# Re-ordering the queues of a fused convolution and two-layer product: multiplications of the taps, the order of the adds, the seeds of the next step, and the list of the first product

## The chip, the cores and the metric

The kernel runs on one core of a Trainium2 chip. Five engines matter. PE multiplies matrices and writes to PSUM; VectorE (DVE) adds, subtracts and transposes; ScalarE (ACT) copies, scales and applies the activation; GpSimd (POOL) adds and issues DMAs that accumulate; SyncE (SP) issues the other DMAs. Each engine works through its own queue in the order in which the program emitted the instructions, and waits on semaphores for the others. The metric is the device time of one execution in microseconds (us), lower is better; the time shown for a kernel is the median of its runs.

## The reference

```python
# x: (8, 4096, 192), weight: (8, 7), w_in: (192, 2048), w_out: (2048, 192), all float32
w = softmax(weight, axis=-1)                      # 7 taps for each of 8 heads
out = sum over k of w[h, k] * x_pad[b, s + k, h, :]  # causal: 6 zeros ahead of x
x = out.reshape(32768, 192)
h = x @ w_in
g = h * (1 / (1 + exp(-1.702 * h)))
return g @ w_out                                  # (32768, 192)
```

A causal convolution with seven taps is followed by two matrix products with a sigmoid-gated activation between them.

## The kernel before, in words

**Steps.** The 32768 rows are worked off in 32 steps (`big`), each of two times 512 rows from two halves of the batch. In step `big` the kernel does the first product and the second product of that step, and beside them it prepares the convolution of step `big + 2`. Steps 2 to 29 have all of this; step 0 is written out apart (`first_step`), step 1 has lists of its own (`FILL_1`), and the last two steps have no convolution left to prepare.

**First product** (`hidden`, L763, called with `v` = 0 and `v` = 1). It does not multiply block by block: 20 products (`TERMS`) replace 24, at the price of sums and copies. `FIRST` (L643) is the list of this work, written out by hand: a `prod` is four matrix instructions (L595, two halves of 64 rows in two passes each), a `copy` is two ACT copies of 128x512 (L630), a `sum` is two DVE additions or subtractions (L636), a `gelu` is two ACT activations from PSUM (L612) or one from SBUF (L617). Names a0 to a9 stand for pairs of PSUM banks, of which there are four; a pair is taken from a list of free ones when its name first occurs and put back at its last use. Names k0 to k6 stand for the five buffers `room`, by the table `ROOM_OF` (L658, one row for each `v`). An item marked 1 or 2 in front belongs to the next half: with `v` = 0 it is work for `v` = 1, with `v` = 1 it is work for the next step. For those of mark 1 that means: they are kept in `later` and emitted when the next step begins (`rest_ahead`, L733), so the order of products on PE in a step is 0, 4, 10, 6, 2, 13, 18, then the list for `v` = 0 with 14, 17, 3, 16, 1 and so on, then the list for `v` = 1. The first of them, the copy of a0 to a2, is the seed of the next step: product 0 adds to that copy. It is emitted still within the second product, where `PLAN` has `final` (`final`, L1315, through `seeds_ahead`, L725).

**Fillers.** `FILL` (L660) says between which items of `FIRST` other work is emitted: `add` (POOL additions of 128x512 of a multiplied tap to the convolution, `next_add` L501), `turn` (DVE transposes of x), `vsum` (POOL sums of blocks of the convolution, L363 and L361), `g` (DVE sums of blocks of g), `cross` (SP DMAs that copy blocks of the convolution to the other 64 rows, L523). At the first `turn` all adds that are left are emitted, and the DMA `cross` of one block.

**Second product** (`second`, L1002). 20 main products with four steps each (two for one of them) are worked through in 78 rounds (`go`, L1036); a round is three matrix instructions of the main product and one of a side product, in two passes, so eight instructions of L1020. `PLAN` (L954) is the list, in which the rounds stand between everything else: `sum` (DVE, 128x1024, L361 and L363), `acc` (POOL DMAs that accumulate, L996), `seed` (ACT copy 96x256, L1049), `join` (DVE 96x256), `turn` (DVE transpose, L935), `store` (SP, L946), `tap` (one ACT multiplication of x by a tap, 128x512, L487), `tree` (POOL DMAs that add up the taps of one third of the columns, L509). When a side product is complete, ACT copies it out of PSUM at once (32x256, L1045). 21 taps are multiplied in a step; those of two thirds of the columns are added by the 12 POOL additions of the next step, in the order in which they were multiplied (first in, first out).

**What sets the order.** Nothing is planned at run time. Emission order is queue order on each engine, and an instruction waits for the last writers and readers of what it touches. At the boundary of two steps the program emits, in this order: side copy after round 74, two more rounds, the seed (`final`), two rounds, the last side copy, then `rest_ahead` with product 0, product 4, the copy of a2 to k2, product 10, the copy of a0 to k6, the sum that makes a4, and so on.

Of the kernel before, what the change touches and what calls it, by code (L numbers as in the profile page):

```python
# [15 lines left out]
def kernel(  # L16
# [80 lines left out]
    g = consts.tile([P, NG, 2, 2, NG, T], F32)  # L97
# [401 lines left out]
    tree, adds = [], []  # L499

    def next_add():  # L501
        if adds:
            dst, home = adds.pop(0)
            nc.gpsimd.tensor_add(dst, dst, home)  # L504

    def add_taps():
# [57 lines left out]
    def prepare(big):  # L564

        for k in range(K if big < 3 else 0):
            yield "", 0.76 if k else 0.48, lambda k=k: conv(big, 1, k)
        yield f"conv {big}", 0.0, lambda: None
        def done():
            need(f"taps {big}")  # L570
            while adds:
                next_add()
            if OPEN_SUM:
                sums_c(big, *OPEN_SUM)
            cross(big, OPEN, OPEN + 1)

        yield f"done {big}", 0.0, done
# [60 lines left out]
    def plain(u, m, n, v, slot, ks=range(NC), first=0):  # L638

        for k in ks:  # L640
            product1(slot, NC * (2 * u + m) + k, 2 * k + n, 0, v, k == first)

    FIRST = [  # L643
# [13 lines left out]
    ]  # L657
    ROOM_OF = ((0, 4, 1, 1, 4, 4, 4), (3, 0, 2, 2, 0, 2, 1))  # L658

    FILL = [  # L660
        {
            1: (("add", 4), ("add", 4), ("add", 4)), 9: (("turn", 0),), 15: (("turn", 1),), 21: (("turn", 2),),
        },
        {
            0: (("vsum",), ("vsum",), ("vsum",), ("vsum",)), 1: (("vsum",),), 2: (("vsum",),), 3: (("g", 0),),
            12: (("g", 1),), 13: (("g", 2), ("vsum",)), 17: (("g", 3), ("vsum",), ("vsum",)), 18: (("g", 4),),
            20: (("vsum",),), 26: (("vsum",),),
        },
    ]
    FILL_1 = [  # L670
        {
            0: (("add", 12),), 7: (("work", 0.8),), 10: (("tap",), ("work", 0.8)), 13: (("tap",),),
            15: (("work", 0.8),), 19: (("tap",),), 25: (("work", 0.8),), 29: (("work", 0.8), ("tap",)),
            32: (("work", 0.8),), 35: (("tap",),), 36: (("tap",),), 40: (("tap",),), 42: (("work", 0.8),),
        },
        {
            3: (("g", 0),), 13: (("g", 1),), 16: (("g", 2),), 17: (("g", 3),), 22: (("g", 4),), 29: (("turn", 0),),
            31: (("turn", 1),), 35: (("turn", 2),),
        },
    ]  # L680

# [9 lines left out]
    def do(big, v, half, kind, *args):  # L691
# [7 lines left out]
        def at(name):  # L699
            return where[name] if name[0] == "a" else rooms[ROOM_OF[v][int(name[1:])]]  # L700

# [236 lines left out]
    def store(big, n, o=None, queues=(nc.sync,) * 3):  # L938
# [13 lines left out]
        (6, 6, "-", 10), (0, 5, "+", 6), (8, 8, "+", 0), (1, 7, "-", 6), (1, 1, "-", 11),  # L952
    ]
    PLAN = [  # L954
        ("sum", 14, 14, "-", 18), ("side", 13, 16, "k0"), ("main", 1, 5, "p2", 1), ("vsum",), ("cross",), ("go", 3),
# [16 lines left out]
        ("main", 9, 6, "p4", 0), ("vsum",), ("go", 1), ("tap",), ("tap",), ("tap",), ("go", 2),  # L972
        ("join", "k9", "p1", "+", "k5"), ("go", 1), ("join", "k10", "p0", "-", "k9"), ("main", 3, 15, "p2", 0),
        ("go", 1), ("acc", 18, 14), ("tree",), ("go", 1), ("seed", "p1", "k1", 1), ("sum", 5, 7, "+", 15), ("go", 2),
        ("main", 21, 7, "p2", 0), ("tap",), ("tap",), ("tap",), ("go", 1), ("sum", 6, 14, "+", 6), ("go", 1),
        ("side", 7, 20, "k1"), ("vsum",), ("vsum",), ("tree",), ("go", 1), ("tap",), ("go", 1), ("sum", 6, 6, "-", 17),
# [13 lines left out]
        ("turn", 1, 1, 0, "k8"), ("store", 1, 0),  # L990
    ]

    def sum_g(dst, a, op, b=None):
# [358 lines left out]
```

## Time and profile before

| what | value |
| --- | --- |
| median of three runs | 2308.58 us (2307.7 to 2309.06) |
| the profiled execution | 2306.48 us |
| its span, first to last instruction | 2304.7 us |
| PE busy | 2267.7 us, 98% |
| DVE busy | 1935.8 us, 84% |
| ACT busy | 1779.9 us, 77% |
| POOL busy | 1069.3 us, 46% |
| granted TensorE clock | 0.998 |
| copies of side products, ACT L1045 | 364 ns each, 651 of them |
| taps, ACT L487 | 714 ns each, 534 in the largest group |
| adds of taps, POOL L504 | 1312 ns each, 354 of them |

The span is what the engines need from the first to the last instruction; 1.78 us of the profiled execution's time lie around it. Busy time is a share over the whole execution, and PE is busy nearly always. In such a kernel the shares say little. What counts is where PE is late, by how much in one step, and who let it go, since the same pattern is repeated in 28 steps. In a line of the timeline stand the start, the busy time, the engine, the line of the code, the operation, what it writes and reads, the shapes, the count, and in brackets how long the engine idled before it and who released it. In the chain of waits stand the pieces of work that set the end, with start and length.

### The profile page before, as it was taken

The page shows a single profiled execution, that of the slowest core. Times are in us where ns is not written, and L with a number is a line of the kernel's source. Part 1 is how long each engine was busy: PE and PEld are TensorE (multiplying, and loading weights), DVE is VectorE, ACT ScalarE, POOL GpSimd, SP SyncE. Part 2 cuts the span into 40 slices and gives each one's busy share as a digit, 9 for nine tenths or more (in the row PEclk, how much of TensorE's full clock was granted, in tenths as well). Part 3 has the DMA queues.
Part 4 walks back from the last instruction along what each step waited for, and adds up shares of the span by engine and source line. Part 5 has one row for each costly group of instructions (what it writes and reads, how often), then busy time and mean ns, then how long its engine had stood idle before and what let it go on. Part 6 is the DMA issues. An engine that isn't in the chain of part 4 may idle for free.

```text
span 2304.7 us, 62266 instructions
## 1 busy us (share of the span) xinstructions
PE 2267.7 (98%) x24966; PEld 1343.7 (58%) x24966; DVE 1935.8 (84%) x2842; ACT 1779.9 (77%) x3481; POOL 1069.3 (46%) x1101
## 2 busy tenths in 40 slices
PE   9899999999999999999999999999999999999999
PEld 4356556665556556566565566565556555655655
DVE  8798888888888888888888888788888788888788
ACT  8578877778777788777788777887777877778755
POOL 1446544555444554535554445555355544455510
PEclk9999999999999999999999999999999999999999
DMA  8876667666676666676666766666766667664543
GB/s 199 156 150 134 130 118 154 128 127 124 126 139 135 132 123 131 119 150 130 126 130 122 140 138 128 123 129 119 152 127 126 128 119 147 135 131 97 101 96 70
DMA packets 281073, 298.85 MB, mean 130 GB/s; under 512 B 120144, under 2 KB 212304, under 8 KB 280784
## 3 DMA queue, kind: packets, MB, share of 16 engines
q0 software_dynamic: 58080, 151.48, 36.5%
q1 hardware_dynamic: 221056, 143.00, 27.6%
q8 instruction: 197, 3.23, 0.6%
q14 instruction: 92, 0.75, 0.1%
q10 hardware_dynamic: 1648, 0.39, 0.1%
HBM read 53.15 MB, written 25.17 MB: 34 GB/s over the span
## 4 chain that ended last, share of the span: by engine, by line
PE 82%; ACT 11%; DVE 5%; issue 2%; DMA 1%; SPq 0%; POOL 0%; DVEq 0%; ACTq 0%; POOLq 0%
PE slot L595 47%; PE slot L1020 34%; ACT g L487 6%; ACT room L1045 2%; PE slot L837 1%; DVE g L363 1%; DVE slot L361 1%; ACT room L1049 0%; DMA conv_t<-conv_t 0%; DVE g L361 0%; DVE room L361 0%; ACT slot L1049 0%; ACT g L612 0%; DVE room L363 0%; DMA osbs<-in_moe_w_out_dram 0%
## 5 line engine op out<-in xcount | busy, mean ns | idle before, releaser
L595 PE MATMUL slot<-conv_t,w_in_s 64*128 64x512 f32 x5152 | 1159.6, 598 | 12.6 <-issue 8.1
L595 PEld LDWEIGHTS slot<-conv_t,w_in_s 64*128 64x128 f32 x5152 | 700.8, 186 | 460.5 <-issue 209.7
L1020 PE MATMUL slot<-g,w_form 128*32 128x256 f32 x9672 | 900.1, 379 | 0.3 <-DVE room L363 0.3
L1020 PEld LDWEIGHTS slot<-g,w_form 128*32 128x32 f32 x9672 | 482.1, 110 | 160.2 <-DVE room L363 0.8
L636 DVE TENSOR_TENSOR slot<-slot,room 128x512 f32<-128x512 f32 x496 | 321.7, 694 | 205.6 <-ACT g L612 132.1
L612 ACT ACTIVATE g<-slot 128x512 f32<-128x512 f32 x776 | 429.2, 610 | 78.9 <-PE slot L595 78.6
L1020 PE MATMUL slot<-g,w_out_s 128*32 128x256 f32 x5952 | 468.1, 380 | 9.5 <-DVE slot L361 5.6
L504 POOL TENSOR_TENSOR conv_t<-conv_t,g 128x512 f32<-128x512 f32 x354 | 463.1, 1312 | 23.1
L363 DVE TENSOR_TENSOR g<-g 128x1024 f32<-128x1024 f32 x372 | 449.6, 1229 | 5.3
L1045 ACT COPY room<-slot 32x256 f32<-32x256 f32 x651 | 236.8, 364 | 252.2 <-PE slot L1020 242.4
L630 ACT COPY room<-slot 128x512 f32<-128x512 f32 x620 | 340.2, 597 | 65.1 <-PE slot L595 34.1
L1020 PEld LDWEIGHTS slot<-g,w_out_s 128*32 128x32 f32 x5952 | 237.1, 110 | 210.2 <-ACT g L617 23.5
L487 ACT ACTIVATE g<-xt,cw 128x512 f32<-128x512 f32 x534 | 347.7, 714 | 3.7
L509 POOL DMA_DIRECT2D g<-g x120 | 120.8, 1025 | 322.4 <-DVE room L361 140.9
L996 POOL DMA_DIRECT2D g<-g x124 | 116.2, 937 | 295.2 <-DVE g L363 209.7
L363 POOL TENSOR_TENSOR conv_t<-conv_t 128x256 f32<-128x256 f32 x210 | 163.2, 787 | 185.6 <-PE slot L595 185.3
L1020 PE MATMUL slot<-osbs,w_form 128*32 128x256 f32 x2232 | 227.3, 379 | 0.2 <-ACT room L1049 0.2
L636 DVE TENSOR_TENSOR slot<-room,slot 128x512 f32<-128x512 f32 x248 | 159.7, 690 | 26.6 <-PE slot L595 24.3
L630 ACT COPY slot<-slot 128x512 f32<-128x512 f32 x248 | 135.7, 576 | 41.2 <-PE slot L595 40.2
L636 DVE TENSOR_TENSOR room<-slot,room 128x512 f32<-128x512 f32 x248 | 159.1, 682 | 5.3 <-ACT room L630 2.1
L617 ACT ACTIVATE g<-room 128x1024 f32<-128x1024 f32 x124 | 132.7, 1070 | 38.2 <-DVE room L636 38.2
L1020 PEld LDWEIGHTS slot<-osbs,w_form 128*32 128x32 f32 x2232 | 113.9, 110 | 42.7 <-ACT room L1049 0.6
(171 smaller groups left out, 1744.2 us busy)
## 6 DMA issues: line engine op xcount, KB each, us to landing
g<-g POOLq DMA_DIRECT2D x124, 512.0 KB, 5.8
xin<-in_x_dram SPq DMA_DIRECT2D x240, 180.0 KB, 4.1
conv_t<-conv_t SPq DMA_DIRECT2D x186, 192.0 KB, 2.9
g<-g POOLq DMA_DIRECT2D x120, 256.0 KB, 5.5
out_dram<-osbs SPq DMA_DIRECT2D x186, 128.0 KB, 2.5
conv_t<-conv_t SPq DMA_DIRECT2D x124, 128.0 KB, 2.3
g<-room POOLq DMA_DIRECT2D x31, 512.0 KB, 5.1
conv_t<-g POOLq DMA_DIRECT2D x60, 256.0 KB, 6.0
```

The lines of the kernel that those rows point to most:

```text
L363: eng.tensor_sub(v(dst), v(a), v(b))
L487: act.mul(home, conv_src(big, c, k), cw[:, c, k : k + 1])
L504: nc.gpsimd.tensor_add(dst, dst, home)
L509: nc.gpsimd.dma_start(out=out, in_=src, accum_op=ALU.add)
L595: nc.tensor.matmul(slot[h], w_in_s[halves[h], a, v * P : (v + 1) * P], src, start=first, stop=True, skip_group_check=True,)
L612: act.activation(dst[:, :, h, :], src[h].rearrange("p (o t) -> p o t", o=2), AF.Gelu_apprx_sigmoid, scale=float(sign),)
L617: act.activation(dst.rearrange("p o h t -> p h o t"), src.rearrange("p h (o t) -> p h o t", o=2), AF.Gelu_apprx_sigmoid, scale=float(sign),)
L630: act.copy(bank(dst, h), bank(src, h))
L636: op(*(bank(t, h) for t in (dst, a, b)))
L996: nc.gpsimd.dma_start(out=spot(dst), in_=spot(a), accum_op=ALU.add)
L1020: nc.tensor.matmul(dst, w, t, start=first, stop=last, skip_group_check=True)
L1045: act.copy(to, d)
```

## The change

Five things change, all of them positions in lists. The instructions are the same in number, shape and kind.

1. `next_add` takes the last entry of the list of adds and not the first. The POOL additions of a step come in the opposite order: the tap that was multiplied last is added first.
2. In `FIRST` products 5 and 19 change places, the copy to k3 and the activation of a7 change places, and the sum that makes a3 stands at the head of the list. By the order in which names take free bank pairs, a3 then takes the pair that a9 left and a1 the one that a0 left, where it was the other way round.
3. `ROOM_OF` puts k5 of `v` = 0 into buffer 1 (it was 4) and k6 of `v` = 1 into buffer 4 (it was 1).
4. `FILL` and `FILL_1` place adds, transposes of x, sums of blocks, and sums of g elsewhere. The first sum of g for `v` = 1 comes behind the sum that makes a3. One `cross` moves from `PLAN` to `FILL`.
5. In `PLAN` the taps are placed anew, DVE sums and POOL accumulations move by some rounds, and `final` stands two rounds earlier, behind round 74, with the last tap behind it.

```diff
-            dst, home = adds.pop(0)
+            dst, home = adds.pop()
...
-        (0, "prod", 1, "a1"), (0, "gelu", 1, 0, "a5", 1), (0, "prod", 15, "a6"), (0, "prod", 7, "a4"),
-        (0, "copy", "a7", "a6", 1), (0, "gelu", 1, 1, "a4", 1), (0, "prod", 19, "a6"),
-        (0, "sum", "a8", "a1", "-", "k2"), (0, "prod", 5, "a7"), (0, "prod", 12, "a8"), (0, "copy", "k3", "a6", 1),
-        (0, "sum", "k4", "a8", "+", "k3"), (0, "gelu", 0, 1, "a7", 1), (2, "prod", 11, "a0"),
...
+        (0, "sum", "a3", "a4", "-", "k1"), (0, "gelu", 2, 1, "a0", 1), (0, "copy", "k0", "a2", 1),
+        (0, "prod", 14, "a1"), (0, "prod", 17, "a3"), (0, "sum", "a5", "k1", "-", "a1"), (0, "gelu", 3, 1, "a3", 1),
...
+        (0, "prod", 15, "a6"), (0, "prod", 7, "a4"), (0, "gelu", 1, 0, "a5", 1), (0, "copy", "a7", "a6", 1),
+        (0, "prod", 5, "a7"), (0, "prod", 19, "a6"), (0, "gelu", 1, 1, "a4", 1), (0, "gelu", 0, 1, "a7", 1),
+        (0, "sum", "a8", "a1", "-", "k2"), (0, "prod", 12, "a8"), (2, "prod", 11, "a0"), (0, "copy", "k3", "a6", 1),
...
-    ROOM_OF = ((0, 4, 1, 1, 4, 4, 4), (3, 0, 2, 2, 0, 2, 1))
+    ROOM_OF = ((0, 4, 1, 1, 4, 1, 4), (3, 0, 2, 2, 0, 2, 4))
...
-            1: (("add", 4), ("add", 4), ("add", 4)), 9: (("turn", 0),), 15: (("turn", 1),), 21: (("turn", 2),),
+            0: (("add", 4),), 6: (("add", 4),), 7: (("turn", 0),), 9: (("add", 4),), 21: (("turn", 1),),
+            26: (("turn", 2),),
...
-            0: (("vsum",), ("vsum",), ("vsum",), ("vsum",)), 1: (("vsum",),), 2: (("vsum",),), 3: (("g", 0),),
+            0: (("vsum",),), 1: (("vsum",), ("vsum",)), 2: (("g", 0),), 6: (("vsum",), ("vsum",)), 8: (("vsum",),),
...
-        ("main", 9, 6, "p4", 0), ("vsum",), ("go", 1), ("tap",), ("tap",), ("tap",), ("go", 2),
+        ("main", 9, 6, "p4", 0), ("vsum",),
+        ("tap",), ("go", 2), ("tap",), ("go", 1), ("join", "k9", "p1", "+", "k5"), ("tree",), ("go", 1),
...
-        ("main", 21, 7, "p2", 0), ("tap",), ("tap",), ("tap",), ("go", 1), ("sum", 6, 14, "+", 6), ("go", 1),
+        ("sum", 5, 7, "+", 15), ("go", 1), ("main", 21, 7, "p2", 0), ("tap",), ("tap",), ("tap",), ("tap",), ("go", 1),
...
-        ("store", 0, 0), ("main", 24, 19, "p5", 0), ("go", 2), ("final",), ("join", "k1", "p3", "-", "k3"), ("go", 1),
+        ("turn", 1, 0, 0, "k6"), ("store", 0, 0), ("main", 24, 19, "p5", 0), ("final",), ("tap",), ("go", 2),
+        ("join", "k1", "p3", "-", "k3"), ("go", 1), ("join", "k2", "p2", "-", "k4"), ("turn", 0, 0, 1, "k1"),
```

On ACT, behind the side copy after round 42, the order was: five taps, two side copies, a seed, three taps, a side copy, a tap, a side copy, the seed k5, four taps, a side copy, a tap, a side copy, four taps, two side copies, the two copies of `final`, the last side copy. It becomes: three taps, a side copy, a tap, a side copy, a seed, four taps, two side copies, the seed k5, four taps, two side copies, four taps, a side copy, a tap, a side copy, the two copies of `final`, a tap, the last side copy.

More of the change, by code (lines that the diff above doesn't have):

```diff
@@ L643 @@
     FIRST = [
[13 rows of a table removed]
[12 rows of a table added]
     ]
-    ROOM_OF = ((0, 4, 1, 1, 4, 4, 4), (3, 0, 2, 2, 0, 2, 1))
+    ROOM_OF = ((0, 4, 1, 1, 4, 1, 4), (3, 0, 2, 2, 0, 2, 4))
     FILL = [
         {
-            1: (("add", 4), ("add", 4), ("add", 4)), 9: (("turn", 0),), 15: (("turn", 1),), 21: (("turn", 2),),
-        },
-        {
-            0: (("vsum",), ("vsum",), ("vsum",), ("vsum",)), 1: (("vsum",),), 2: (("vsum",),), 3: (("g", 0),),
-            12: (("g", 1),), 13: (("g", 2), ("vsum",)), 17: (("g", 3), ("vsum",), ("vsum",)), 18: (("g", 4),),
-            20: (("vsum",),), 26: (("vsum",),),
+            0: (("add", 4),), 6: (("add", 4),), 7: (("turn", 0),), 9: (("add", 4),), 21: (("turn", 1),),
+            26: (("turn", 2),),
+        },
+        {
+            0: (("vsum",),), 1: (("vsum",), ("vsum",)), 2: (("g", 0),), 6: (("vsum",), ("vsum",)), 8: (("vsum",),),
+            12: (("vsum",),), 14: (("g", 1),), 15: (("g", 2),), 17: (("vsum",), ("vsum",)), 18: (("g", 3),),
+            21: (("vsum",),), 23: (("g", 4),), 25: (("vsum",),), 35: (("cross",),),
         },
@@ L671 @@
         {
-            0: (("add", 12),), 7: (("work", 0.8),), 10: (("tap",), ("work", 0.8)), 13: (("tap",),),
-            15: (("work", 0.8),), 19: (("tap",),), 25: (("work", 0.8),), 29: (("work", 0.8), ("tap",)),
-            32: (("work", 0.8),), 35: (("tap",),), 36: (("tap",),), 40: (("tap",),), 42: (("work", 0.8),),
-        },
-        {
-            3: (("g", 0),), 13: (("g", 1),), 16: (("g", 2),), 17: (("g", 3),), 22: (("g", 4),), 29: (("turn", 0),),
-            31: (("turn", 1),), 35: (("turn", 2),),
+            0: (("add", 12),), 4: (("tap",),), 6: (("work", 0.8),), 15: (("work", 0.8),), 16: (("work", 0.8),),
+            21: (("tap",),), 23: (("tap",),), 25: (("tap",), ("work", 0.8), ("work", 0.8)), 28: (("work", 0.8),),
+            32: (("tap",),), 35: (("tap",),), 38: (("tap",),), 42: (("work", 0.8),),
+        },
+        {
+            0: (("g", 0),), 6: (("g", 1),), 19: (("g", 2), ("g", 3)), 23: (("g", 4),), 25: (("turn", 0),),
+            28: (("turn", 1),), 31: (("turn", 2),),
         },
@@ L954 @@
     PLAN = [
-        ("sum", 14, 14, "-", 18), ("side", 13, 16, "k0"), ("main", 1, 5, "p2", 1), ("vsum",), ("cross",), ("go", 3),
[16 rows of a table removed]
-        ("main", 9, 6, "p4", 0), ("vsum",), ("go", 1), ("tap",), ("tap",), ("tap",), ("go", 2),
-        ("join", "k9", "p1", "+", "k5"), ("go", 1), ("join", "k10", "p0", "-", "k9"), ("main", 3, 15, "p2", 0),
-        ("go", 1), ("acc", 18, 14), ("tree",), ("go", 1), ("seed", "p1", "k1", 1), ("sum", 5, 7, "+", 15), ("go", 2),
-        ("main", 21, 7, "p2", 0), ("tap",), ("tap",), ("tap",), ("go", 1), ("sum", 6, 14, "+", 6), ("go", 1),
-        ("side", 7, 20, "k1"), ("vsum",), ("vsum",), ("tree",), ("go", 1), ("tap",), ("go", 1), ("sum", 6, 6, "-", 17),
[13 rows of a table removed]
-        ("turn", 1, 1, 0, "k8"), ("store", 1, 0),
+        ("sum", 14, 14, "-", 18), ("side", 13, 16, "k0"), ("main", 1, 5, "p2", 1), ("sum", 7, 8, "-", 7), ("vsum",),
[18 rows of a table added]
+        ("sum", 5, 7, "+", 15), ("go", 1), ("main", 21, 7, "p2", 0), ("tap",), ("tap",), ("tap",), ("tap",), ("go", 1),
+        ("tree",), ("go", 1), ("sum", 6, 14, "+", 6), ("side", 7, 20, "k1"), ("vsum",), ("vsum",), ("go", 1),
[6 rows of a table added]
+        ("main", 15, 12, "p2", 0), ("tap",), ("tap",), ("tap",), ("tree",), ("go", 1), ("tap",), ("go", 1),
[3 rows of a table added]
+        ("turn", 1, 0, 0, "k6"), ("store", 0, 0), ("main", 24, 19, "p5", 0), ("final",), ("tap",), ("go", 2),
[3 rows of a table added]
     ]
```

72 rows, old and new, of tables (FIRST, PLAN) are left out of this document.

## The prediction

> **What bounds the kernel now.** I read the page first: busy shares, then the chain of waits.
>
> ```profile
> span 2304.7 us, 62266 instructions
> PE 2267.7 (98%) x24966; PEld 1343.7 (58%) x24966; DVE 1935.8 (84%) x2842; ACT 1779.9 (77%) x3481; POOL 1069.3 (46%) x1101
> PE 82%; ACT 11%; DVE 5%; issue 2%; DMA 1%; SPq 0%; POOL 0%; DVEq 0%; ACTq 0%; POOLq 0%
> ```
>
> The change adds no work to PE and takes none away, so only PE's lateness can move. The chain in order of time, over the whole execution (start, length, what), gives the period:
>
> ```profile
> 108.44 14.99 PE slot L595 x55
> 187.18 35.72 PE slot L595 x153
> 257.46 35.76 PE slot L595 x153
> ...
> 544.37 3.61 DMA conv_t<-conv_t
> ...
> 1032.75 35.76 PE slot L595 x153
> 1103.07 35.76 PE slot L595 x153
> ...
> 2196.45 33.81 PE slot L1020 x624
> ```
>
> A steady step takes 1103.07 - 1032.75 = 70.32 us: 35.76 us of first product, then the second. The 78 rounds of a second product without convolution beside it took 33.81 us, 0.433 us a round. The same chain at the end of one step:
>
> ```profile
> 998.19 18.37 PE slot L1020 x336
> ...
> 1024.86 0.44 DVE slot L361
> 1025.30 0.04 issue
> 1025.35 7.11 PE slot L1020 x128
> 1032.46 0.29 issue
> 1032.75 35.33 PE slot L595 x152
> ```
>
> From 998.19 to 1032.75 are 34.56 us, 0.75 us more than 33.81. Two places carry most of it: round 62, which waited for a DVE join, and the start of the first product. Both hang on ACT. Its timeline there (start, busy, what, idle before):
>
> ```profile
> 1016.58 0.37 ACT L1045 COPY room<-slot 32x256 f32<-32x256 f32 x1 [0.47 <-PE slot L1020]
> 1016.97 3.18 ACT L487 ACTIVATE g<-xt,cw 128x512 f32<-128x512 f32 x5
> 1020.06 0.74 ACT L1045 COPY room<-slot 32x256 f32<-32x256 f32 x2
> ...
> 1021.09 1.95 ACT L487 ACTIVATE g<-xt,cw 128x512 f32<-128x512 f32 x3
> ...
> 1024.46 0.37 ACT L1049 COPY room<-slot 96x256 f32<-96x256 f32 x1
> 1024.73 2.56 ACT L487 ACTIVATE g<-xt,cw 128x512 f32<-128x512 f32 x4
> ...
> 1032.08 1.06 ACT L630 COPY slot<-slot 128x512 f32<-128x512 f32 x2
> 1033.16 0.36 ACT L1045 COPY room<-slot 32x256 f32<-32x256 f32 x1
> 1033.88 1.07 ACT L630 COPY room<-slot 128x512 f32<-128x512 f32 x2 [0.35 <-PE slot L595]
> 1035.54 1.07 ACT L630 COPY room<-slot 128x512 f32<-128x512 f32 x2 [0.59 <-DVE room L361]
> ```
>
> From the side copy after round 42 (1016.58) to the last side copy (until 1033.52) no row has an idle time: ACT is full for 17 us. The seed k5 (1024.46) frees the join at 1024.86, and that frees PE. The seed of the next step (1032.08) frees the first product at 1032.75, 0.67 us after its start. Only before the copy of a2 to k2 (1033.88) is there a gap, 0.35 us, in which ACT waits for product 0.
>
> **The change part by part.** All sums are per step, in the times of this step.
>
> *Taps and seed (`PLAN`).* The taps behind round 42 are the same 18. One leaves the stretch ahead of the seed: the last, which now follows it. A tap takes 0.62 us in the queue (five from 1016.97 to 1020.06). Against that, the side copy after round 50 now meets PE: round 50 ends at 998.19 + 50 x 0.433 = 1019.84, and the copy can start 0.2 us later (as at 1016.58, after round 42 at 1016.38). Three taps, a copy and a tap end at about 1019.9, so ACT waits 0.1 us. And taps and copies alternate oftener; each change costs up to 0.1 us (a copy follows a tap by 0.61 to 0.73 us), 0.1 in all. The seed starts 0.62 - 0.10 - 0.11 = 0.41 us earlier, at 1031.67, and the first product at 1032.34. The seed k5 comes 0.4 us earlier too (1024.05), its join ends at 1024.9, before round 62 is due (998.19 + 62 x 0.433 = 1025.04): that stall goes. Round 78 then ends at about 1032.0, so ACT still sets the start of the first product. Gain 0.41 us.
>
> Next in ACT's queue stand the two seed copies (until 1032.73), the last tap (until 1033.4) and the last side copy (until 1033.75). The copy to k2 could start 1033.88 - 1032.75 = 1.13 us after the first product, at 1033.47; it starts at 1033.8, 0.34 us late. Product 10, third in the queue, overwrites what this copy reads, with one product between. That is a loss of 0.34 us. What was hidden in the gap of 0.35 us is the last tap's cover, and it is used up. Net 0.41 - 0.34 = 0.07 us gained. The cause is plain: ACT has the same work between round 42 and the copy to k2 in both orders, so at most the gap of 0.35 us plus the change of waits can be gained.
>
> *Last tap added first.* The rows of DVE and POOL at this boundary (timeline of each), and of DVE one step on:
>
> ```profile
> 1033.56 1.89 DVE L361 TENSOR_TENSOR room<-room 96x256 f32<-96x256 f32 x1 [0.15 <-ACT room L1045]
> 1036.16 1.30 DVE L636 TENSOR_TENSOR slot<-slot,room 128x512 f32<-128x512 f32 x2 [0.23 <-PE slot L595]
> ```
>
> ```profile
> 1033.58 7.06 POOL L504 TENSOR_TENSOR conv_t<-conv_t,g 128x512 f32<-128x512 f32 x5
> ```
>
> ```profile
> 1103.89 0.42 DVE L361 TENSOR_TENSOR room<-room 96x256 f32<-96x256 f32 x1 [0.16 <-ACT room L1045]
> ```
>
> The last join, which reads SBUF twice, takes 0.42 us alone and 1.89 us when the first POOL add starts beside it. Before, the add's start hung on the `tree` DMAs and fell anywhere; now it cannot start before the last tap ends (1033.4), and the join cannot before the last side copy ends (1033.75). So the add stands ahead of the join in nearly every step, and the join ends near 1035.4, as in the step shown. Behind it on DVE stands the last transpose, behind that the last store on SP and the `cross` of block 5, and on ACT the copy to k6 (1035.54 in the step shown, 0.59 us of waiting), behind which product 13 waits. In the step shown all that cost PE nothing. Bounds: 0 (this step), and 0.3 us, should the 0.34 us by which product 10 comes later not cover product 13's sum as well. I take 0.05 for the copy to k6. For the `cross`:
>
> ```profile
> 1037.40 1.24 SPq L523 DMA_DIRECT2D conv_t<-conv_t  x2
> ```
>
> ```profile
> conv_t<-conv_t SPq DMA_DIRECT2D x124, 128.0 KB, 2.3
> ```
>
> Its second DMA is issued at 1038.05 and lands after 2.3 us, 1040.35. Product 3, the tenth, needs it at 1032.75 + 9 x 0.894 = 1040.8 (35.76 / 40 = 0.894). A late landing costs: the chain's row at 544.37 is one. Since the late join now comes in every step, I take 0.10 us a step, between 0 and 0.3. Freeing homes of taps in the other order costs nothing: the adds are done some 17 us after the step's start (12 x 1.4), before the activations of `v` = 1 overwrite the rest.
>
> *`FIRST`, `ROOM_OF`.* Products 5 and 19 both need the copy to a7 to be through, so the wait at that place stays; k3 and the activation of a7 exchange places and end together. With k5 and k6 in other buffers a DVE sum no longer waits for an activation, nor a copy for a DVE sum, but ACT is full there and PE does not wait. Nothing; bounds -0.1 and 0.1. The transposes behind other sums: 0.77 us each, DVE idles longer.
>
> *`FILL`: the sum of g behind the sum that makes a3.* DVE and POOL in `v` = 1:
>
> ```profile
> 1054.57 1.22 DVE L363 TENSOR_TENSOR g<-g 128x1024 f32<-128x1024 f32 x1
> 1056.26 1.30 DVE L636 TENSOR_TENSOR slot<-slot,room 128x512 f32<-128x512 f32 x2 [0.47 <-PE slot L595]
> 1057.53 1.29 DVE L636 TENSOR_TENSOR slot<-room,slot 128x512 f32<-128x512 f32 x2
> 1059.24 1.29 DVE L636 TENSOR_TENSOR slot<-room,slot 128x512 f32<-128x512 f32 x2 [0.42 <-PE slot L595]
> ...
> 1064.67 1.31 DVE L363 TENSOR_TENSOR osbs<-osbs,g 128x1024 f32<-128x1024 f32 x1
> ```
>
> ```profile
> 1056.39 0.73 POOL L363 TENSOR_TENSOR conv_t<-conv_t 128x256 f32<-128x256 f32 x1 [3.63 <-PE slot L595]
> 1057.20 1.52 POOL L361 TENSOR_TENSOR conv_t<-conv_t 128x256 f32<-128x256 f32 x2
> ...
> 1064.97 2.40 POOL L361 TENSOR_TENSOR conv_t<-conv_t 128x256 f32<-128x256 f32 x2
> ```
>
> The sum of g (1054.57) ran while DVE had nothing else to do. Now a3 comes first, then g, then a5. The sum at 1059.24 waits for product 3, the 30th of 40, and the copy at 1033.88 for product 0, the first: (1059.24 - 1033.88) / 29 = 0.874 us a product. Product 13, which a3 needs, is the 26th and through at 1059.24 - 4 x 0.874 = 1055.74; a3's bank pair is free by then, where before it was not until 1056.26. So a3 at 1055.8, g at 1057.0 (two halves at 0.6), a5 at 1058.15 (1.14 from g's start to the next), done at 1059.45 instead of 1058.82. Product 16, the 31st, needs a5; it starts when product 3 ends, near 1059.2, and needs the second half near 1059.6. With the sum of POOL that ends at 1057.12 beside g, 0.1 us more (as at 1064.67: 1.31 for 1.22). That is on the edge: bounds 0 and 0.75 (when g also waits for the next POOL sum of 0.73). I take 0.10 us. The other rows speak for the lower end: at 1064.97 it was POOL that gave way.
>
> The Trainium skill ("SBUF — State Buffer", "Who interferes with whom") says that a DVE instruction with two SBUF inputs and a GpSimd instruction that reads SBUF exclude each other, and that the one issued first keeps the port. The rows at 1064.67 and 1064.97 agree; the join at 1033.56, 0.02 us ahead of the add and yet held up, does not. By this rule the sum of g would be held up by at most the rest of the first POOL sum, and the term would be 0.1 us.
>
> *Step 1* has other lists: it takes 187.18 - 108.44 = 78.7 us, 8.4 more than a steady one. I take 0, with 3 us to either side.
>
> **Sum.** Steps 2 to 29, 28 of them: -0.07 + 0.05 + 0.10 + 0.10 = +0.18 us, times 28 = +5.0 us. On the profiled execution (2306.48 us, of which 1.78 lie around the span) that gives 2311.5; the median of the runs is 2.1 us above it, so 2308.58 + 5.0 = 2313.6 us.
>
> **The rivals.** (1) Faster: the late copy to k2 turns out hidden, because products 0 and 4 leave more room than I count. Then 0.41 us a step stays, 28 x 0.41 = 11.5 us: 2297.1 us. The full queue on ACT speaks against it, the removed stall at round 62 for it. It decides from 0.17 us a step. (2) No change: the exchange on ACT nets 0.07 us and no new wait appears: 2308.58 - 2.0 = 2306.6 us. The step shown, which bore the late join at no cost, speaks for it. (3) Slower by far: the sum of g loses to two POOL sums and product 16 waits 0.75 us: 28 x 0.75 = 21 us, less 2: 2327.6 us. For it speaks that the join at 1033.56 lost to an add that started later; against it 1064.97.
>
> **How the numbers follow.** My forecast has 0.40, with its own range 2309 to 2319; rival 1 0.20, rival 2 0.22, rival 3 0.18. A measurement tells 0.2% (4.6 us) from no change. Faster: rival 1 and a little, 0.22. The same: rival 2 and the lower part of my forecast, 0.32. Slower: 0.46. The range reaches from 2299 (most of rival 1) to 2329 (rival 3).
>
> **What would show it.** In the chain, the DVE piece at round 62 should be gone and the first product should follow the second some 0.4 us earlier; the copy to k2 should show no idle time ahead of it, where 0.35 us stood; the last join should take 1 to 1.9 us in nearly every step; the first sum of g in `v` = 1 should last 1.2 to 1.35 us. I am wrong if product 10 does not wait, if g takes 2 us, or if `cross` of block 5 lands late in many steps.

## The result, and the profile after

The kernel after took 2299.92 us in the median of seven runs (2299.38 to 2301.22), against 2308.57 us for the kernel before (seven runs, 2304.02 to 2309.38): a ratio of 0.9967, 95% interval 0.9956 to 0.9979. That is 8.65 us less, where 5.0 us more was forecast. The profiled execution took 2299.75 us, 6.73 us less than the one of before. The page of the kernel after, its span, busy times and the shares of its chain:

```profile
span 2298.0 us, 62000 instructions
PE 2271.9 (99%) x24966; PEld 1377.8 (60%) x24966; DVE 1921.3 (84%) x2842; ACT 1775.9 (77%) x3481; POOL 1100.6 (48%) x1101
PE 94%; DVE 2%; DMA 1%; ACT 1%; issue 1%; SPq 0%; DVEq 0%; ACTq 0%
```

ACT's share of the chain fell from 11% to 1%, DVE's from 5% to 2%. The chain in order of time (start, length, what) shows how a step now looks:

```profile
257.05 36.23 PE slot L595 x156
293.29 33.81 PE slot L1019 x624
...
995.75 33.81 PE slot L1019 x624
...
1029.73 36.23 PE slot L595 x156
1065.97 33.81 PE slot L1019 x624
...
1099.95 36.23 PE slot L595 x156
...
2189.87 33.81 PE slot L1019 x624
2223.68 35.51 PE slot L595 x153
```

Three readings. First, the second product with convolution beside it takes 33.81 us, as the one without did; before, it took 34.56 - 0.29 = 34.27. The DVE piece at round 62 is gone. From its start to the first product are now 33.98 us instead of 34.56: 0.58 us gained. Second, the first product takes 36.23 us instead of 35.76: 0.47 us lost inside a PE row, where the chain shows no wait. Third, the steady period is 1099.95 - 1029.73 = 70.22 us instead of 70.32: 0.10 us gained, 2.8 us in 28 steps.

The rest of the 6.7 us comes from steps that took longer than the usual one. Steps 3 to 30 took 2223.68 - 257.05 = 1966.6 us, against 2196.45 + 33.81 - 257.46 = 1972.8 before: 6.2 us. (Another 0.41 us had been gained when step 3 began, at 257.05 instead of 257.46. Step 30 has no taps beside it, so it has the loss and not the gain: 36.23 + 33.81 = 70.04 us.) From the starts of PE's instructions in both traces I took the time from each first product to the next, steps 3 to 29:

| us | before | after |
| --- | --- | --- |
| median step | 70.34 | 70.22 |
| mean step | 70.48 | 70.24 |
| longest step | 71.66 | 70.50 |
| steps over 0.05 above the median | 11 of 27 | 3 of 27 |
| of these, product 3 late for block 5 | 5 | 0 |
| last round to first product | 0.67 | 0.55 |
| loss at products 10 and 6, third and fourth in the queue | 0.00 | 0.42 (0.35 + 0.07) |
| loss behind the sum that makes a3 | 0.00 | 0.05 |

So the mean step gained 0.24 us: 0.10 in every undisturbed step, 0.14 from late steps, most of which are gone. One of these, step 7 in the chain of before, with the products of that step from the view of the tile:

```profile
539.73 2.12 DVE room L361
...
543.79 0.54 SPq L523
544.33 0.04 issue
...
548.03 4.13 PE slot L595 x17
```

```profile
L595 PE MATMUL slot<-conv_t,w_in_s x56: 589/589/693, 538.9 to 552.0; 64*128 64x512 f32 x56
```

The first product of this step began at 538.9. In a step without such a wait, product 3 follows 7.94 us later, here at 546.84. The last join had taken 2.12 us, and the second DMA of the `cross` was issued at 544.37 and landed at 547.98, 1.14 us too late. The join explains little of it: that DMA was issued 5.46 us after the start of the step, and in the same step of the kernel after 5.30 us, where it landed in time. What differs is its flight, 3.61 us against 2.00. From the view of the DMAs for the time of its flight (queue: packets, MB, share of the engines; issues: KB each, us to landing), first before and then after:

```profile
q8 instruction: 1, 0.02, 2.2%
conv_t<-conv_t SPq DMA_DIRECT2D x1, 64.0 KB, 3.6
```

```profile
conv_t<-conv_t SPq DMA_DIRECT2D x1, 64.0 KB, 2.0
```

Before, a packet of 16 KB of the profile's instruction queue was in flight beside the copy; after, it began only when the copy had landed (7.53 us after the start of the step, the landing at 7.30). In all five late steps of before (7, 18, 23, 24, 29) such a packet lay in the flight of a copy of block 5, and that copy took 3.2 to 3.6 us. (In steps 24 and 29 it was the first of the two copies, and the second was issued 1.75 and 2.08 us behind it instead of some 0.6.)

At the boundary after, on ACT, DVE, POOL and SP (timelines: start, busy, what, idle before):

```profile
1017.54 0.37 ACT L1044 COPY room<-slot 32x256 f32<-32x256 f32 x1 [0.23 <-PE slot L1019]
...
1029.07 1.06 ACT L630 COPY slot<-slot 128x512 f32<-128x512 f32 x2
1030.15 0.72 ACT L487 ACTIVATE g<-xt,cw 128x512 f32<-128x512 f32 x1
1030.90 0.36 ACT L1044 COPY room<-slot 32x256 f32<-32x256 f32 x1
1031.29 1.07 ACT L630 COPY room<-slot 128x512 f32<-128x512 f32 x2
1032.59 1.07 ACT L630 COPY room<-slot 128x512 f32<-128x512 f32 x2 [0.23 <-DVE room L361]
```

```profile
1031.29 1.21 DVE L361 TENSOR_TENSOR room<-room 96x256 f32<-96x256 f32 x1 [0.78 <-ACT room L1044]
```

```profile
1030.96 9.29 POOL L504 TENSOR_TENSOR conv_t<-conv_t,g 128x512 f32<-128x512 f32 x7 [0.63 <-ACT g L487]
```

```profile
1034.46 1.19 SPq L523 DMA_DIRECT2D conv_t<-conv_t  x2
```

The seed (1029.07) stands ahead of the tap (1030.15). The copy to k2 (1031.29) has no idle time ahead of it: it starts 1031.29 - 1029.73 = 1.56 us after the first product, where 1.13 would have done. These 0.43 us are as large as the loss at products 10 and 6. The last join starts 0.33 us after the first add and takes 1.21 us.

### The profile page after: what moved, and what is told of

Same layout as the page of the kernel before. It is cut to its first block, busy times and chain, and to the rows that moved or that the text cites. A ratio compares the mean times of both kernels' runs of the same rounds, so it can differ in the third digit from the quotient of the medians.

```text
span 2298.0 us, 62000 instructions
## 1 busy us (share of the span) xinstructions
PE 2271.9 (99%) x24966; PEld 1377.8 (60%) x24966; DVE 1921.3 (84%) x2842; ACT 1775.9 (77%) x3481; POOL 1100.6 (48%) x1101
## 4 chain that ended last, share of the span: by engine, by line
PE 94%; DVE 2%; DMA 1%; ACT 1%; issue 1%; SPq 0%; DVEq 0%; ACTq 0%
PE slot L595 48%; PE slot L1019 44%; PE slot L837 1%; DMA g<-in_moe_w_in_dram 1%; DVE g L363 0%; DVE g L361 0%; PE slot L842 0%; SPq L266 0%; DMA xin<-in_x_dram 0%; ACT g L612 0%; DMA w_in_s<-in_moe_w_out_dram 0%; ACT g L487 0%; DMA conv_t<-conv_t 0%; ACT room L630 0%; ACT w_form L487 0%
## 5 line engine op out<-in xcount | busy, mean ns | idle before, releaser
L595 PEld LDWEIGHTS slot<-conv_t,w_in_s 64*128 64x128 f32 x5152 | 728.0, 186 | 440.3 <-issue 218.6
L504 POOL TENSOR_TENSOR conv_t<-conv_t,g 128x512 f32<-128x512 f32 x354 | 452.6, 1282 | 66.8 <-ACT g L487 43.8
L612 ACT ACTIVATE g<-slot 128x512 f32<-128x512 f32 x776 | 421.1, 613 | 77.7 <-PE slot L595 77.5
L363 DVE TENSOR_TENSOR g<-g 128x1024 f32<-128x1024 f32 x372 | 442.8, 1224 | 1.1
L363 POOL TENSOR_TENSOR conv_t<-conv_t 128x256 f32<-128x256 f32 x210 | 193.5, 929 | 232.1 <-PE slot L595 186.7
L995 POOL DMA_DIRECT2D g<-g x124 | 107.6, 943 | 352.3 <-PE slot L1019 166.6
L509 POOL DMA_DIRECT2D g<-g x120 | 104.5, 886 | 224.4 <-DVE room L363 88.5
L636 DVE TENSOR_TENSOR slot<-room,slot 128x512 f32<-128x512 f32 x248 | 156.3, 684 | 14.7 <-PE slot L595 13.7
L361 DVE TENSOR_TENSOR room<-room 96x256 f32<-96x256 f32 x155 | 87.4, 564 | 71.1 <-ACT room L1044 70.0
```

What stands on the lines that cost most here:

```text
L363: eng.tensor_sub(v(dst), v(a), v(b))
L509: nc.gpsimd.dma_start(out=out, in_=src, accum_op=ALU.add)
L595: nc.tensor.matmul(slot[h], w_in_s[halves[h], a, v * P : (v + 1) * P], src, start=first, stop=True, skip_group_check=True,)
L612: act.activation(dst[:, :, h, :], src[h].rearrange("p (o t) -> p o t", o=2), AF.Gelu_apprx_sigmoid, scale=float(sign),)
L636: op(*(bank(t, h) for t in (dst, a, b)))
L995: nc.gpsimd.dma_start(out=spot(dst), in_=spot(a), accum_op=ALU.add)
```

## The experiments

My theory after the result was this: `PLAN` alone made the gain, by getting work of ACT from ahead of the seed to behind it; it paid 0.42 us of it back at the copy to k2; and what made the sum come out as a clear gain was that block 5 no longer landed late. The rivals: the order of the adds did it, by making the boundary regular; or the new lists of the first product (`FIRST`, `FILL`, `ROOM_OF`) did it; or it was the seed, emitted two rounds earlier. Times of before beside the runs below: 2307.1 to 2307.3 us in the median.

**The order of the adds.** Kernel after, first in, first out again:

```diff
-            dst, home = adds.pop()
+            dst, home = adds.pop(0)
```

> The changed kernel with the adds first in, first out again. Theory: the order of the adds is worth nothing in itself: 2299 to 2301 us; the last join is held up by an add already running, for 0.4 to 1.7 us instead of 1.2 in every step, and no product waits for it. Rival A: 2303 to 2305 us, with late DMAs of block 5 in several steps.

2299.9 us, ratio 0.9969 (0.9958 to 0.998), the step 70.22 us as in the kernel after. What the order did do is seen in the trace: the last join ends 1.98 to 3.05 us after the first product begins, instead of 2.77 in every step. No product waits for it. This rival falls.

**`PLAN` alone, and all but `PLAN`.** Kernel before with the new `PLAN`, kernel after with the old one:

```diff
-    PLAN = [...]  # the whole list of before
+    PLAN = [...]  # the whole list of after
```

> The kernel before with the new PLAN alone (taps, DVE sums, seed); adds in the old order, old FIRST, ROOM_OF and FILL. Theory: the new PLAN carries the gain. The first product starts 0.57 us earlier in each of 28 steps and product 10 gives 0.42 us back, 0.15 us a step, 4 us in all; and because product 3 then comes 0.42 us later after the step's start, the DMA of block 5 is hardly ever late, another 2 to 5 us: 2300 to 2303 us, at or a little under the changed kernel's step (70.2 us). Rival A, the regular start of the adds carries the gain: about 2304 to 2308 us, with steps of more than 70.6 us left. Rival B, the first product's lists carry it: 2308 us.

> The changed kernel with the old PLAN; adds last first, new FIRST, ROOM_OF and FILL. Theory: 2308 to 2311 us; round 62 waits again for 0.38 us, steps of 70.36 us (70.32 and 0.05 for the sum of g behind a3), late DMAs of block 5 as before. Rival A: about 2303 us, since the adds keep their new order. Rival B: about 2300 us.

The first took 2478.22 us, 1.0741 (1.0727 to 1.0756). The new `PLAN` has five `cross` and the old one six, because the change moved one to `FILL`. Without it, the blocks shift by one, and block 3 too is copied only behind the last stores. The waits of PE in this kernel (total, times, longest):

```profile
PE slot L595 <- DMA conv_t<-conv_t: 98.4, 29, 4.2
```

The second kernel had seven `cross`, so block 5 went ahead of the stores: 2304.96 us, 0.9992 (0.9983 to 1.0001). The granted clock of the first was 0.97, where the other kernels here show 0.996 to 0.999; what it lost beyond the 98.4 us of that row was not followed further. Both times lie outside what was expected, and neither is a trial of `PLAN` alone; both were run again with the count of `cross` kept. Kernel before with the new `PLAN`:

```diff
     PLAN = [...]  # the whole list of after, and in its first line:
-        ("sum", 14, 14, "-", 18), ("side", 13, 16, "k0"), ...
+        ("cross",), ("sum", 14, 14, "-", 18), ("side", 13, 16, "k0"), ...
```

> The kernel before with the new PLAN and one more cross at its head, so that as many DMAs stand ahead of the stores as before; adds in the old order, old FIRST, ROOM_OF and FILL. Theory: steps of 70.17 us (the gain at the seed 0.57 us, the loss at products 4 and 10 0.42 us, no loss behind a3), and 2299 to 2301 us, since product 3 comes later and the DMA of block 5 is rarely late. Rival A, the order of the adds carries the gain: 2303 us or more. Rival B, the lists of the first product carry it: 2307 us.

2299.66 us, 0.9968 (0.9955 to 0.9981): the whole gain. Its chain has the same second product (33.82 us) and 36.18 us of first product:

```profile
962.33 36.18 PE slot L595 x154
998.51 33.81 PE slot L1019 x624
1032.32 0.17 issue
1032.49 36.18 PE slot L595 x154
```

Kernel after with the old `PLAN`, and without the `cross` of `FILL`:

```diff
-            21: (("vsum",),), 23: (("g", 4),), 25: (("vsum",),), 35: (("cross",),),
+            21: (("vsum",),), 23: (("g", 4),), 25: (("vsum",),),
```

> The changed kernel with the old PLAN and without the cross that its FILL took over, so that the DMA of block 5 stands behind the stores again. Theory: all of the gain was in PLAN and in that DMA: steps of 70.37 us with late landings, 2307 to 2310 us. Rival: the lists of the first product and the adds are worth 2 us or more by themselves: 2305 us or less.

2306.51 us, 0.9996 (0.9987 to 1.0006), a step of 70.37 us. By the times, the gain is in `PLAN`, and the lists of the first product with the order of the adds are together worth nothing that can be told from no change.

For the late landings the two profiles say something else, and against what was expected. With the old `PLAN`, product 3 is due 7.94 us after the start of the step, as before, and yet block 5 never held it up by more than 0.05 us; the steps longer than the usual 70.37 us lost their time at other products. With the new `PLAN` in the kernel before it is due 8.36 us after the start, and was late in two steps, by 1.09 and 0.48 us. So the gain of the undisturbed step is shown to be `PLAN`'s. That the late landings go with `PLAN` is not shown.

**Which edit in `PLAN`.** Kernel before with the seed two rounds earlier, and the same with the last tap behind it:

```diff
-        ("store", 0, 0), ("main", 24, 19, "p5", 0), ("go", 2), ("final",), ("join", "k1", "p3", "-", "k3"), ("go", 1),
+        ("store", 0, 0), ("main", 24, 19, "p5", 0), ("final",), ("go", 2), ("join", "k1", "p3", "-", "k3"), ("go", 1),
```

> The kernel before with the seed (final) emitted two rounds earlier and nothing else. Theory: ACT's queue keeps its order and is full up to there, so nothing moves: steps of 70.32 us, 2306 to 2309 us. Rival: the emission two rounds earlier is what brings the first product forward: 0.3 us a step or more, 2298 us or less.

```diff
-        ("join", "k7", "k7", "+", "k3"), ("tap",), ("tap",), ("go", 1), ("join", "k2", "k2", "-", "k1"),
+        ("join", "k7", "k7", "+", "k3"), ("tap",), ("go", 1), ("join", "k2", "k2", "-", "k1"),
...
-        ("store", 0, 0), ("main", 24, 19, "p5", 0), ("go", 2), ("final",), ...
+        ("store", 0, 0), ("main", 24, 19, "p5", 0), ("final",), ("tap",), ("go", 2), ...
```

> The kernel before with the seed two rounds earlier and one tap, the last, behind it. Theory: the seed comes 0.6 us earlier, the first product 0.36 us (then round 78 sets it, as round 62 still waits), and the copy to k2 about 0.2 us late: 0.1 to 0.2 us a step, 2302 to 2305 us. Rival, the gain at the seed needs the new places of all the taps: 2306 to 2309 us.

The seed alone: 2306.92 us, 0.9999 (0.9989 to 1.0009), a step of 70.33. Its position among the rounds says nothing while ACT's queue is full; what stands ahead of it on ACT is the same. With the tap behind it: 2305.43 us, 0.9989 (0.998 to 0.9999), just above what was expected. Its undisturbed steps, 12 of 27, take 70.12 to 70.14 us, 0.19 less than before and 0.09 less than in the kernel after. But the median is 70.21 and the mean 70.39, since product 3 came late in seven steps. The waits of PE, of the seed alone and then with the tap:

```profile
PE slot L595 <- issue: 8.1, 28, 0.3
PE slot L1020 <- DVE slot L361: 5.6, 28, 0.2
```

```profile
PE slot L1020 <- DVE slot L361: 5.6, 28, 0.2
PE slot L595 <- DMA conv_t<-conv_t: 1.1, 2, 0.6
```

The row at the start of the first product (28 times, 0.3 us) goes with the tap; the row at round 62 stays, and goes only with the rest of the new `PLAN`. So one tap behind the seed gives the undisturbed step more than the whole gain. What the kernel after gains on top, round 62's wait, it pays back at products 10 and 6, where it loses 0.42 us and this kernel 0.17. The late landings decide how much of the gain is seen.

**Late landings, measured by themselves.** Kernel before, the last `cross` ahead of the stores on SP:

```diff
-        ("store", 0, 0), ("main", 24, 19, "p5", 0), ("go", 2), ("final",), ("join", "k1", "p3", "-", "k3"), ("go", 1),
+        ("cross",), ("store", 0, 0), ("main", 24, 19, "p5", 0), ("go", 2), ("final",), ("join", "k1", "p3", "-", "k3"), ("go", 1),
```

> The kernel before with one edit: the DMA of block 5 to the other rows is issued ahead of the stores and not behind them. Theory: the steps of more than 70.32 us in the kernel before (70.4 to 71.7, 3.9 us in all in its profile) come from late landings of that DMA, so they go: 2303 to 2305 us, nearly every step 70.32 us. Rival: they come from the join that the adds hold up, or from elsewhere: 2307 to 2309 us.

2304.0 us, 0.9989 (0.998 to 0.9998): 3.1 us less. Product 3 was late in no step. The usual step stayed (70.33), the mean fell from 70.48 to 70.38 and the longest from 71.66 to 70.72. The waits for block 5 were worth some 3 us of the kernel before.

**The sum of g.** Kernel after, the first sum of g for `v` = 1 ahead of the sum that makes a3 again:

```diff
-            0: (("vsum",),), 1: (("vsum",), ("vsum",)), 2: (("g", 0),), 6: (("vsum",), ("vsum",)), 8: (("vsum",),),
+            0: (("g", 0), ("vsum",)), 1: (("vsum",), ("vsum",)), 6: (("vsum",), ("vsum",)), 8: (("vsum",),),
```

> The changed kernel with the first sum of g ahead of the sum that makes a3 again. Theory: the 0.05 us that product 17 or 16 lost in the second half of the first product goes: 28 x 0.05 = 1.4 us, 2298.5 us. Rival, the loss there comes from the bank pairs and not from g: 2299.9 us.

2299.07 us, 0.9963 (0.995 to 0.9975). The time alone can't be told from the kernel after; the chain can, since its row repeats to 0.01 us: the first product takes 36.18 us instead of 36.23, so the moved sum cost 0.05 us a step. Product 3 was late in one step of this profile, by 0.43 us: that it was late in none of the kernel after is in part luck.

**The loss at the copy to k2.** Kernel after, with the last tap emitted in the next step, behind the copy to k6, and the adds in the order in which their taps are then ready:

```diff
...
-            dst, home = adds.pop()
+            _, _, dst, home = adds.pop(min(range(len(adds)), key=lambda i: ADDS.index(adds[i][:2])))
...
+            if list(item[:2]) == ["copy", "k6"] and big > 1:
+                while ready:
+                    next_tap()
...
-        ("turn", 1, 0, 0, "k6"), ("store", 0, 0), ("main", 24, 19, "p5", 0), ("final",), ("tap",), ("go", 2),
+        ("turn", 1, 0, 0, "k6"), ("store", 0, 0), ("main", 24, 19, "p5", 0), ("final",), ("go", 2),
...
```

> The changed kernel with the last tap of a step emitted behind the copy of a0 to k6 in the next step, and not ahead of the last side copy; its add stays the first, then those of the other third. Theory: product 10 lost 0.42 us because the last tap stood ahead of the copy to k2; that goes, so 28 x 0.42 = 11.8 us less, but product 3 comes 0.42 us earlier, so the DMA of block 5 is late at times, 0 to 4 us back: 2288 to 2292 us. Rival, ACT is as late there without the tap: 2299 to 2301 us.

2287.83 us, 0.9916 (0.9902 to 0.9929). ACT and the chain of this kernel:

```profile
1026.41 0.36 ACT L1049 COPY room<-slot 32x256 f32<-32x256 f32 x1
1027.12 2.05 ACT L631 COPY room<-slot 128x512 f32<-128x512 f32 x4 [0.35 <-PE slot L596]
1029.04 0.75 ACT L487 ACTIVATE g<-xt,cw 128x512 f32<-128x512 f32 x1
```

```profile
992.00 33.81 PE slot L1024 x624
1025.82 0.17 issue
1025.99 35.80 PE slot L596 x155
```

The copy to k2 starts 1027.12 - 1025.99 = 1.13 us after the first product, with ACT idle again for 0.35 us ahead of it. The first product is back at 35.80 us: 0.43 us of loss gone, and the gain of 0.58 us at its start kept. Product 10 lost its 0.42 us to the tap ahead of the copy; the other 0.05 of the 0.47 us are the sum of g, by the trial above.

**A version that beats both.** The last kernel with the sum of g and the last `cross` moved as in the two trials above; then with a second tap in the next step, behind the copy to k0:

```diff
...
-            0: (("add", 4),), 6: (("add", 4),), 7: (("turn", 0),), 9: (("add", 4),), 21: (("turn", 1),),
+            0: (("add", 4),), 3: (("tap",),), 6: (("add", 4),), 7: (("turn", 0),), 9: (("add", 4),), 21: (("turn", 1),),
...
```

> The kernel with the last tap behind the copy to k6, and beside it the DMA of block 5 ahead of the stores and the first sum of g ahead of a3. Theory: 28 x (0.42 + 0.05) = 13.2 us less than the changed kernel and no late DMA: 2286 to 2287 us, steps of 69.75 us. Rival as for the tap alone: 2298 us.

> As the run before, with the last two taps of a step in the next one: one behind the copy to k6, one behind the copy to k0. Theory: the seed's copy starts 0.6 us earlier, ahead of the end of round 78, so PE and not ACT sets the start of the first product: up to 0.24 us a step and 0.12 us of product 0, 28 x 0.36 = 10 us less: 2276 to 2280 us. Rival, the taps are only in the way of the activations in the first product: 2287 us or more.

The first took 2287.54 us, 0.9912 (0.9899 to 0.9926), the second 2279.01 us (2277.92 to 2280.72), 0.9877 (0.9864 to 0.9891). The second's chain:

```profile
985.84 33.81 PE slot L1023 x624
1019.65 35.72 PE slot L596 x157
1055.38 33.82 PE slot L1023 x624
1089.19 35.72 PE slot L596 x157
```

The piece of 0.17 us ahead of the first product is gone: the seed no longer waits in ACT's queue, so PE alone sets the boundary, and the period is 69.54 us. The chain shows no wait at either end of the first product.

## Why the prediction was wrong

*Which of its steps held.* The order of work was read rightly. The seed moved ahead of a tap, round 62's wait went, the first product came earlier (0.58 us; I had 0.41), ACT had no idle time ahead of the copy to k2, and product 10 waited (0.42 us; I had 0.34). The first rival, in which this delay is hidden, did not come about: the first product grew by 0.47 us. `FIRST` and `ROOM_OF` cost nothing, as said. The adds' order cost nothing either (I had 0.05 for the copy to k6). All the signs that the prediction named came as it said, and none of its signs of being wrong: they tested the order of work, and not the sign of the `cross` term. One reading was wrong without effect: step 1 does not begin at 108.44, where a piece of its first product stands in the chain, but by PE's starts at 96.09; it took 91.05 us, and 90.57 after.

*Taps and seed, the net.* Predicted 0.07 us gained a step, measured 0.58 - 0.42 = 0.16. Both terms were undersized. The tap was worth its 0.62 us. The wait behind round 50, for which I took 0.10, was 0.23 us (ahead of 1017.54). But the 0.11 us for more changes between taps and copies were wrong: by the two lists in the section on the change there are six groups of taps in both orders, and the stretch from behind the seed k5 to the seed of the next step took 1029.07 - 1021.84 = 7.23 us (the first tap behind the seed k5 starts at 1021.84), where it had taken 1032.08 - 1024.73 = 7.35. My rule for the net, that ACT has the same work up to the copy to k2 in both orders, so that no more than the gap of 0.35 us and the change of waits can be won, held.

*The sum of g.* Predicted 0.10, measured 0.05. The sum was not held up:

```profile
1053.18 1.30 DVE L636 TENSOR_TENSOR slot<-slot,room 128x512 f32<-128x512 f32 x2 [1.11 <-ACT room L630]
1054.38 1.23 DVE L363 TENSOR_TENSOR g<-g 128x1024 f32<-128x1024 f32 x1
1055.54 2.48 DVE L636 TENSOR_TENSOR slot<-room,slot 128x512 f32<-128x512 f32 x4
```

```profile
1054.61 2.39 POOL L361 TENSOR_TENSOR conv_t<-conv_t 128x256 f32<-128x256 f32 x2
```

g started 0.23 us ahead of the two POOL sums and took 1.23 us; POOL took 2.39 us for what took 1.52 us before. The third rival needed g to lose; here it was POOL.

*The `cross` of block 5: the step that failed.* I booked 0.10 us a step lost, "since the late join now comes in every step". Measured are 0.14 us gained by fewer late steps, 0.12 of them at block 5. Three things were wrong in it. I priced the join at the 1.89 us that it took when it started 0.02 us ahead of the add; with the add 0.33 us ahead of it, it took 1.21 us, and ended 2.77 us after the first product's start, where in before the slowest had ended at 2.95. I took the due time of product 3 from before, though by my own sum product 10 came later, and product 3 with it: it is now due 8.36 us after the first product's start, not 7.94, so the loss at k2 bought slack for the DMA. And I did not look at how often block 5 was late before: it delayed product 3 in 5 of 27 steps, and made 0.12 of the 0.16 us by which the mean (70.48) exceeded the usual step (70.32). This was what could be gained. In the 20 steps for which the landing is recorded, block 5 lands 7.27 to 8.03 us after the first product's start in the kernel after (median 7.30), always before 8.36; before it was 6.69 to 9.07 (median 7.29) against 7.94.

*The sum.* In the usual step -0.16 + 0.05, 0.10 us gained to the rounding of the rows, where the same terms gave me -0.07 + 0.05 + 0.10 = 0.08 lost. Over the steps -0.24 instead of +0.18 us. Of the miss of 13.7 us, 0.24 x 28 = 6.7 are the `cross`, booked with the wrong sign; the three mis-sized terms (taps and seed 0.09, copy to k6 0.05, sum of g 0.05) are 0.19 x 28 = 5.3. The last 1.7 us are about what the medians differ by more than the two profiled executions (8.65 against 6.73).

*What stays open.* The late landings were worth some 3 us, by the trial with the early `cross`. Why they went is not settled. The later product 3 covers part of it: the five delays of before, 0.15, 0.21, 0.47, 0.65 and 1.00 us, would shrink to 0, 0, 0.05, 0.23 and 0.58 with 0.42 us more time (an estimate from these rows). The order of the adds is not needed: with first in, first out in the kernel after, product 3 was late in no step. The rest hangs on where the packets of the instruction queue fall. Of the five late copies of before, those of steps 7, 18 and 23 had such a packet beside them, begun 5.71 to 6.71 us after the start of the step; in the kernel after it began at 7.21 to 7.53, when they had landed or were about to. No run moved these packets and nothing else. So it is seen in the traces that the long flights and the packets go together, and not tested that the one makes the other.

## What to carry to other kernels

When work on a full queue is moved from ahead of one reader to behind it, look for the next reader in the same queue and give the moved work a place behind that one too: here the step of the kernel after was 0.10 us shorter with the tap behind the seed, and 0.53 us (69.79 for 70.32) with the tap behind the copy to k6. A cost inside the next stage shows as a longer row of the bound engine, not as a wait, so compare the length of the stage with its floor. And before a transfer is booked as late or on time, take its slack over all steps and with the new due time, not from one step of the old kernel, and look at what else was in flight when it was late.

## What the runs showed of the hardware that was not expected

- A copy of 64 KB from SBUF to SBUF lands in 2.0 us, and in up to 4.1 us when a packet of 16 KB of the instruction queue is in flight beside it; there are 197 such packets in each profile. In nine profiles (before, after and seven of the trials) 71 of the 83 copies of block 5 with such a packet beside them took over 2.4 us, and the other 12 had it only from 1.69 us after the issue on; of those without, 47 of 358 took as long, 31 of them issued early in steps 4, 9, 15, 20 and 25, where they landed in time.
- A DVE join of 96x256 that reads SBUF twice takes 0.42 us alone. When a POOL add of 128x512 runs beside it and has the port, the join ends 0.28 us after the add: 1.21 us when the add of 1.26 us began 0.33 us before it, 1.89 to 2.13 us in the kernel before, where the first add of a step began 0.02 to 0.26 us after it. The Trainium skill ("SBUF — State Buffer", "Who interferes with whom") has the one issued first keep the port. The sum of g at 1054.38, 0.23 us ahead of POOL's, agrees. So do three joins in the kernel after with first in, first out, which began 0.01 to 0.06 us ahead of a later add: they took 0.42 us, and that add 1.49 to 1.54 us instead of 1.27. The join at 539.73, 0.23 us ahead of the add at 539.96, does not. The adds that won though they began later all stood right behind a DMA issue of POOL (here 539.40, for 0.86 us); such an add takes 1.59 us in the profile whether a join stands beside it or not. What in this decides was not tested.

```profile
539.96 12.32 POOL L504 TENSOR_TENSOR conv_t<-conv_t,g 128x512 f32<-128x512 f32 x9
```

- The chain's rows of undisturbed steady stages repeat to 0.01 us (36.23, 33.81), so an edit of 0.05 us a step can be read there where the time itself, with an interval 0.25% wide, can't tell it.
